# Second MLP's first GEMM by Strassen's seven products inside a block, in pairs of tiles

## The chip, the cores and the metric

One core of a Trainium2 chip. The time is that of one execution in device microseconds (us), the median of three runs. TensorE does the matrix products (PE in the profile, PEld for its weight loads); VectorE (DVE), ScalarE (ACT) and GpSimd (POOL) do the elementwise work; SyncE (SP) issues nearly all DMAs, in order, and a DMA that has to wait for a buffer or for data holds up those behind it.

## The reference, cut to what matters

Chunked attention on 4,608 tokens, then two MLPs, all float32. The change is about the second MLP, whose inputs are `x` (4608 x 512), `w_in` (512 x 2048) and `w_out` (2048 x 512):

```
h = x @ w_in
P = a0 + a1*h + a2*h^2 + a3*h^3
Q = 1 + |b0|*|h| + |b1|*h^2
out = (P / (Q + 1e-6)) @ w_out
```

## The kernel before

Every float32 operand of a product is kept as a pair (high part, rest) in TensorE's reduced float32, and each product runs as three matmuls: high by high, high by rest, rest by high (`PASSES`). "A product" below means such three passes.

The 4,608 tokens are nine blocks of 512 columns (`W`). The phases follow one another on TensorE:

* Attention and the first MLP's two input GEMMs: three blocks directly (`cell`), six blocks as three pairs of blocks by Strassen's seven products (`group`, tiles `sa`, `sb`). Attention for later blocks is woven in.
* The output pass of the first MLP: one block directly (tile `a`), eight blocks as four pairs by seven products (tiles `oa`, `ob`), written as 90 items of 12 matmuls. Operands are prepared three items ahead (`LEAD`): ACT takes the high part (L789), DVE the rest (L796).
* The second MLP (from `p2_first`): 144 steps, nine blocks by 16 tiles of 128 rows of h. A step is 12 matmuls 512 columns wide for h (`gemm1`, L428), an elementwise chain on the 128 x 512 tile, and, three steps later, 12 matmuls 512 columns wide of the output GEMM (L956) into four accumulators.

The elementwise chain of a step: ACT squares h (L925), takes |h| (L926) and a3*h+a2 (L927); DVE makes three operations from these (L928 to L930, the last two read h from PSUM); ACT takes a logarithm and an exponential (L936, L937) for the reciprocal; DVE does a Newton step and the product (L938, L939, L940; every tensor operand of these three lies in SBUF, as those of L928 do). Then ACT copies the high part (L945) and GpSimd subtracts to get the rest (L946). All these queues are written out by hand, in program order.

The next block's input is loaded from DRAM in four tiles of 128 x 512, each split by an ACT copy (L583) and a GpSimd subtraction (L584). The 32 tiles of the second MLP's weights are read as 64-bit words and turned into pairs while earlier phases run (`stage`: 18 of them in the Strassen groups, 14 in the output pass), written to DRAM, and read once into eight buffers of 2 MB (`unit2`) at the start of the second MLP, where they stay for all nine blocks. So in that phase next to nothing is loaded. The large buffers are 11 slabs of 16 KB per partition; small tiles of 512 columns come from a ring of 17 (`s2`).

## Time and profile before

| | us |
|---|---|
| time, median of 3 runs (lowest to highest) | 1717.96 (1717.67 to 1718.62) |
| the profiled execution | 1715.83 |
| its span, first to last instruction | 1714.0 |
| TensorE busy | 1681.1 (98%) |
| VectorE busy | 1365.1 (80%) |
| ScalarE busy | 1052.5 (61%) |
| GpSimd busy | 266.1 (16%) |

The mean granted TensorE clock is 0.999 of full speed. The profile's time for a matmul covers more than the distance to the next one, since matmuls overlap; the pace is read from the starts of consecutive groups.

### The profile page before, as it was taken

To read this page: it belongs to the slowest core of one execution; us is meant where nothing else is said; L and a number is where in the kernel's file an instruction comes from. 1 tells how busy PE (TensorE), PEld (TensorE's weight loads), DVE (VectorE), ACT (ScalarE), POOL (GpSimd) and SP (SyncE) were. 2 spreads that over 40 slices of the span, in tenths; PEclk is the share of its full clock that TensorE was granted. 3 is DMA by queue.
4 is the path that set the end of the run, shared out by engine and by line. 5 is a ranking of instruction groups with operands and counts; after the bars stand their busy time and mean duration, and the time that the engine had idled before them with its cause. 6 is when DMAs were issued, how large, how long until landed. Compare 5 with 4: busy or idle time off the path is not lost.

```text
span 1714.0 us, 25378 instructions
## 1 busy us (share of the span) xinstructions
PE 1681.1 (98%) x9600; PEld 1380.6 (81%) x9600; DVE 1365.1 (80%) x1961; ACT 1052.5 (61%) x1687; POOL 266.1 (16%) x258
## 2 busy tenths in 40 slices
PE   6899999999999999999999999999999999999998
PEld 5678877878878878888888888888888888888887
DVE  6868787777778679997885988887878787878786
ACT  6834345555555564565555877676767776767675
POOL 1000000000000000000002323232323232323222
PEclk9999999999999999999999999999999999999999
DMA  7875678877977998468648300010101010101000
GB/s 283 293 236 172 204 240 295 301 280 280 359 281 263 356 345 311 129 216 261 221 144 331 147 27 23 17 33 7 43 7 44 1 50 1 50 1 50 1 25 25
DMA packets 102442, 272.19 MB, mean 159 GB/s; under 512 B 10672, under 2 KB 32176, under 8 KB 97072
## 3 DMA queue, kind: packets, MB, share of 16 engines
q1 hardware_dynamic: 102176, 270.32, 44.5%
q8 instruction: 75, 1.23, 0.3%
q14 instruction: 47, 0.39, 0.1%
q10 hardware_dynamic: 144, 0.26, 0.0%
HBM read 184.55 MB, written 85.98 MB: 158 GB/s over the span
## 4 chain that ended last, share of the span: by engine, by line
PE 58%; issue 2%; POOL 1%; ACT 0%; DVE 0%; POOLq 0%; DVEq 0%
PE o L956 21%; PE h L428 21%; PE oa L889 8%; PE ob L889 6%; PE a L871 2%; POOL ggring L946 1%; POOLq L1054 0%; ACT L986 0%; DVE rring L796 0%; DVE T L930 0%; DVE V L928 0%; ACT R L936 0%; ACT R L937 0%; DVE V L938 0%; DVE V L939 0%
## 5 line engine op out<-in xcount | busy, mean ns | idle before, releaser
L428 PE MATMUL h<-x,w 128*128 128x512 f32 x1728 | 414.9, 389 | 0.9 <-DVE T L930 0.9
L956 PE MATMUL o<-w,ggring 128*128 128x512 f32 x1728 | 414.9, 389 | 0.1
L428 PEld LDWEIGHTS h<-x,w 128*128 128x128 f32 x1728 | 324.3, 188 | 68.6 <-DVE T L930 1.3
L956 PEld LDWEIGHTS o<-w,ggring 128*128 128x128 f32 x1728 | 324.2, 188 | 67.7 <-POOL ggring L946 0.5
L946 POOL TENSOR_TENSOR ggring<-T,ggring 128x512 fp32r<-128x512 f32 x144 | 187.3, 1301 | 517.4 <-ACT ggring L945 292.0
L925 ACT ACTIVATE V<-h 128x512 f32<-128x512 f32 x144 | 85.9, 597 | 170.3 <-PE h L428 169.7
L928 DVE SCALAR_TENSOR_TENSOR V<-V,small,R 128x512 f32<-128x512 f32 x144 | 108.3, 752 | 84.9 <-ACT R L926 84.9
L789 ACT CAST rring<-uring 128x1024 fp32r<-128x1024 f32 x90 | 94.5, 1053 | 87.4 <-PE ob L889 32.7
L938 DVE SCALAR_TENSOR_TENSOR V<-V,R 128x512 f32<-128x512 f32 x144 | 99.9, 694 | 47.0 <-ACT R L937 47.0
L796 DVE TENSOR_TENSOR rring<-uring,rring 128x1024 fp32r<-128x1024 f32 x90 | 109.5, 1221 | 28.6 <-ACT rring L789 27.9
L939 DVE SCALAR_TENSOR_TENSOR V<-V,R 128x512 f32<-128x512 f32 x144 | 123.9, 861 | 4.9
L584 POOL TENSOR_TENSOR x<-x2r,x 128x512 fp32r<-128x512 f32 x36 | 47.9, 1333 | 436.3 <-ACT x L583 433.5
L927 ACT ACTIVATE T<-h,small 128x512 f32<-128x512 f32 x144 | 112.6, 782 | 0.0
L940 DVE SCALAR_TENSOR_TENSOR T<-T,small,V 128x512 f32<-128x512 f32 x144 | 108.3, 752 | 5.1
L428 PE MATMUL g<-xT,w 128*128 128x512 f32 (+1 forms) x444 | 109.1, 391 | 3.1 <-ACT w L104 1.3
L930 DVE SCALAR_TENSOR_TENSOR T<-T,small,h 128x512 f32<-128x512 f32 x144 | 107.7, 748 | 5.1
L465 PE MATMUL sa<-right,left 128*128 128x512 f32 x432 | 109.9, 393 | 0.0
L465 PE MATMUL sb<-right,left 128*128 128x512 f32 x432 | 108.2, 392 | 0.2 <-ACT c L493 0.2
L428 PE MATMUL v<-xT,w 128*128 128x512 f32 (+1 forms) x444 | 107.5, 388 | 0.0
L937 ACT ACTIVATE R<-R,small 128x512 f32<-128x512 f32 x144 | 104.5, 726 | 4.7
L936 ACT ACTIVATE R<-V,small 128x512 f32<-128x512 f32 x144 | 106.0, 736 | 1.6
L945 ACT CAST ggring<-T 128x512 fp32r<-128x512 f32 x144 | 90.0, 625 | 18.3 <-DVE T L940 18.3
(155 smaller groups left out, 2640.6 us busy)
## 6 DMA issues: line engine op xcount, KB each, us to landing
left<-wsd SPq DMA_DIRECT2D x30, 2048.0 KB, 9.8
ud<-u SPq DMA_DIRECT2D x108, 256.0 KB, 3.2
uring<-ud SPq DMA_DIRECT2D x54, 512.0 KB, 5.4
raw<-in_w_dram SPq DMA_DIRECT2D x36, 512.0 KB, 6.4
w<-w2d SPq DMA_DIRECT2D x8, 2048.0 KB, 15.6
wsd<-cb SPq DMA_DIRECT2D x48, 256.0 KB, 2.8
raw<-in_w_dram SPq DMA_DIRECT2D x10, 1024.0 KB, 9.9
wsd<-w SPq DMA_DIRECT2D x36, 256.0 KB, 3.4
```

The source lines that it names most:

```text
L428: nc.tensor.matmul(out=acc[:, ts], lhsT=w[:, wh, wk], rhs=x[:, kk, xh, ts], start=kk == 0 and n == 0, stop=kk == KD - 1 and n == 2,)
L465: nc.tensor.matmul(out=acc, lhsT=lhs[:, wh, kk * P:(kk + 1) * P], rhs=rhs[:, kk, xh, :], start=start and kk == 0 and m == 0, stop=kk == 1 ...
L796: nc.vector.tensor_tensor(out=lo, in0=u_of(t, n, f), in1=hi.bitcast(F32), op=ALU.subtract)
L889: nc.tensor.matmul(out=banks[m][on], lhsT=w[:, wh], rhs=(lo if xh else hi)[:, k], start=fresh and f + k == 0 and p == 0, stop=f + k == KH ...
L927: nc.scalar.activation(out=T, in_=h, func=AF.Identity, scale=a3, bias=a2)
L928: nc.vector.scalar_tensor_tensor(out=V, in0=V, scalar=absb1, in1=R, op0=ALU.mult, op1=ALU.add)
L930: nc.vector.scalar_tensor_tensor(out=T, in0=T, scalar=a1, in1=h, op0=ALU.add, op1=ALU.mult)
L936: nc.scalar.activation(out=R, in_=V, func=AF.Ln, scale=TWO_M63, bias=lnb)
L939: nc.vector.scalar_tensor_tensor(out=V, in0=V, scalar=-2.0, in1=R, op0=ALU.add, op1=ALU.mult)
L940: nc.vector.scalar_tensor_tensor(out=T, in0=T, scalar=a0, in1=V, op0=ALU.add, op1=ALU.mult)
L946: nc.gpsimd.tensor_tensor(out=r[:, 1, :], in0=T, in1=r[:, 0, :].bitcast(F32), op=ALU.subtract)
L956: nc.tensor.matmul(out=acc2[j][m], lhsT=r[:, rh, ms], rhs=wt["q", f][:, wh, :], start=f == 0 and n == 0, stop=f == NF2 - 1 and n == 2,)
```

## The change

* **h in pairs of tiles.** Two neighbouring tiles of h (256 rows) by the block's 512 columns become a 2 x 2 matrix of 128 x 256 pieces; the contraction's 512 rows are cut in two as well. Instead of 24 matmuls 512 wide, a pair takes seven products of 6 matmuls each, 256 wide: 42 matmuls (`products2`). A pair's h lies in two PSUM banks, and there are two such tiles. Some products accumulate in PSUM on others, and three copies on ACT (`both_` twice, `p5`, 256 wide) and two additions on DVE (512 and 256 wide, PSUM in and out) do the rest.
* **The elementwise chain** runs on 1024 columns at a time, once per pair; the copy and subtraction of the output GEMM's operand (`ggring`) stay 512 wide, two each per pair.
* **Order.** TensorE's order is now written by hand too. Iteration p holds the products of pair p, the chain of pair p-1, the operand copies of pair p-2, and the 24 output matmuls of pair p-3 in three lots of eight (`others`): product 0, eight, products 1 to 3, eight, products 4 and 5, eight, product 6.
* **Weights.** `w_in` is kept in DRAM as the seven left operands of each pair of tiles (`wld`, made by `stage_left`, 8 of them: one in the direct cells, seven in the Strassen groups), 1,792 KB for a pair, and `load_lefts` reads them again for each of the 72 pairs into two buffers in turn. The 16 tiles of `w_out` are staged in the output pass (`stage`) and stay in four buffers.
* **The block's input** is loaded as four quarters (`fetch_x2`), turned into seven right operands: four DVE subtractions (`x2_sum`) and seven splits of an ACT copy and a GpSimd subtraction each, 512 columns (`x2_split`), at places in the block's eight iterations that `plan2` lists.
* **Joints.** The first two items' operands of the output pass are prepared in the last turns of the Strassen groups (`open_o`, `start_o`). The last six items of the output pass run as the lots of eight of the first three iterations (`EARLY`, `last_items`), and PSUM is divided once for both.

```diff
+PAIRS = (2, 3, 2)
+EARLY = 3
+BLOCK0 = (
+    (-20, "fetch", 0), (-18, "ring", 0), (-17, "split", 0, "B11"), (-16, "split", 0, "B21"), (-15, "sum", 0, "T1"),
+    (-14, "split", 0, "T1"), (-14, "sum", 0, "T3"), (-12, "ring", 1), (-11, "split", 0, "B22"), (-10, "sum", 0, "T2"),
+    (-10, "split", 0, "T3"), (-9, "split", 0, "T2"), (-9, "sum", 0, "N4"), (-8, "split", 0, "N4"), (-9, "lefts", 0),
+    (-6, "lefts", 1), (-6, "work"), (-3, "lefts", 2), (-3, "quad", 0), (-2, "gg"),
+)
...
+    def stage_left(g):
+        one, two = (raw_tile(4 * g + 2 * n) for n in range(2))
+        yield
+        yield from words_to_whole(*one)
+        yield from words_to_whole(*two)
+        x, y = (w[0].bitcast(F32) for w in (one, two))
...
+        yield from put(0, x, "a")
+        yield from put(6, y[:, W // 2:], "d")
+        a11, a12, a21, a22 = (z[:, k * W // 2:(k + 1) * W // 2] for z in (x, y) for k in range(2))
+        for o, i, j, op in ((a22, a21, a22, ALU.add), (a21, a11, a21, ALU.subtract), (a11, a22, a11, ALU.subtract), (a12, a12, a11, ALU.subtract)):
+            nc.vector.tensor_tensor(out=o, in0=i, in1=j, op=op)
+            yield
+        yield from put(2, x, "s")
+        yield from put(4, y, "u")
...
+    def x2_split(j, name):
...
+        nc.scalar.copy(hi, x)
+        nc.gpsimd.tensor_tensor(out=lo, in0=x, in1=hi.bitcast(F32), op=ALU.subtract)
+
+    def load_lefts(p):
+        parts = (slice(0, 7),)
...
+        if p < 3:
+            ring["lefts", p % 2] = slab(f"lefts{p}", (P, 8, 2, 2 * P))
+            parts = (slice(0, 3), slice(3, 7))
+        for part in parts:
+            nc.sync.dma_start(out=ring["lefts", p % 2][:, part].bitcast(F32), in_=wld[p % NPR][:, part])
...
+    def last_items():
+        for i in range(len(items) - 2 * EARLY, len(items)):
+            prepare(i)
+            todo = list(item_products(i))
+            for n, of in enumerate(todo):
+                nc.tensor.matmul(**of)
+                if n + 1 == len(todo):
+                    item_end(i)
+                yield
...
+        plan2 = ((0, "fetch", None), (2, "split", "B11"), (2, "split", "B22"), (2, "sum", "T1"), (3, "split", "B21"), (3, "sum", "T3"),
+                 (4, "split", "T1"), (4, "sum", "T2"), (5, "split", "T2"), (6, "sum", "N4"), (7, "split", "T3"), (7, "split", "N4"))
+
+        for p in range(NPAIR + 3):
+            a = p if p < NPAIR else None
+            b = p - 1 if 0 <= p - 1 < NPAIR else None
+            c = p - 2 if 0 <= p - 2 < NPAIR else None
+            if a is not None:
+                if p > 1 and p + 1 < NPAIR:
+                    load_lefts(p + 1)
+                tiles[p] = two_banks([P, 2, W], f"h{p}")
+                products2(p, (0,))
+            if b is not None:
...
+                nc.scalar.activation(out=V, in_=H, func=AF.Square)
+            if a is not None:
+                both_ = s2([P, W], f"both{p}")
+                nc.scalar.copy(both_[:, :HW], tiles[p][:, 1, :HW])
+            others(p, 0)
+            if b is not None:
+                nc.scalar.activation(out=R, in_=H, func=AF.Abs, scale=b0)
+                nc.vector.scalar_tensor_tensor(out=V, in0=V, scalar=absb1, in1=R, op0=ALU.mult, op1=ALU.add)
+                nc.scalar.activation(out=T, in_=H, func=AF.Identity, scale=a3, bias=a2)
+                nc.vector.tensor_tensor(out=T, in0=T, in1=H, op=ALU.mult)
+                nc.vector.scalar_tensor_tensor(out=T, in0=T, scalar=a1, in1=H, op0=ALU.add, op1=ALU.mult)
+            if a is not None:
+                products2(p, (1, 2, 3))
+            if c is not None:
...
+                for e in range(2):
+                    es = slice(e * W, (e + 1) * W)
+                    nc.scalar.copy(r[:, 0, es], Tc[:, es])
+                    (nc.vector if c == NPAIR - 1 else nc.gpsimd).tensor_tensor(
+                        out=r[:, 1, es], in0=Tc[:, es], in1=r[:, 0, es].bitcast(F32), op=ALU.subtract
                     )
...
+            if a is not None:
+                nc.scalar.copy(both_[:, HW:], tiles[p][:, 1, :HW])
+                p5 = s2([P, HW], f"p5_{p}")
+                nc.scalar.copy(p5, tiles[p][:, 0, HW:])
+            others(p, 1)
+            if a is not None:
+                products2(p, (4, 5))
+                nc.vector.tensor_tensor(out=tiles[p][:, 0], in0=tiles[p][:, 0], in1=both_, op=ALU.add)
+                nc.vector.tensor_tensor(out=tiles[p][:, 1, HW:], in0=tiles[p][:, 1, :HW], in1=p5, op=ALU.add)
+            if b is not None:
+                nc.scalar.activation(out=R, in_=V, func=AF.Ln, scale=TWO_M63, bias=lnb)
+                nc.scalar.activation(out=R, in_=R, func=AF.Exp, scale=-1.0, bias=expb)
+            others(p, 2)
+            if a is not None:
+                products2(p, (6,))
+            if b is not None:
+                nc.vector.scalar_tensor_tensor(out=V, in0=V, scalar=1.0 + 1e-6, in1=R, op0=ALU.add, op1=ALU.mult)
+                nc.vector.scalar_tensor_tensor(out=V, in0=V, scalar=-2.0, in1=R, op0=ALU.add, op1=ALU.mult)
+                nc.vector.scalar_tensor_tensor(out=T, in0=T, scalar=a0, in1=V, op0=ALU.add, op1=ALU.mult)
```

After these, `plan2`'s entries of the iteration follow, so its splits and sums stand last in the queues of ACT, GpSimd and DVE. At the end of a block (an iteration 2 of the next one) `others` also emits the four evictions of the output (L967, L969 before) and their DMAs, each behind its lot of eight.

## Rows read from the trace of the kernel before

**Rows 1.** Busy time by engine in stretches of 50 us: stretch, engines, clock, DMA share, GB/s.

```profile
600.00:650.00 50.00, 47.89 (x209) 38.58 (x208) 38.50 (x56) 31.44 (x48) 0.00 (x0) 1.00 0.94 343
...
850.00:900.00 50.00, 50.00 (x223) 41.38 (x222) 45.70 (x49) 29.08 (x37) 0.00 (x0) 1.00 0.48 168
...
1300.00:1350.00 50.00, 50.00 (x222) 41.39 (x222) 42.58 (x57) 35.80 (x58) 16.20 (x13) 1.00 0.01 2
```

**Rows 2.** Waits in the second MLP: waiter, releaser, us in total, times, longest.

```profile
PE h L428 <- DVE T L930: 0.9, 1, 0.9
```

**Rows 3.** Timeline of the second MLP, in order of time: start, us, instructions.

```profile
1301.33 1.29 POOL L584 TENSOR_TENSOR x<-x2r,x 128x512 fp32r<-128x512 f32 x1 [0.68 <-PE h L428]
...
1301.50 1.67 DVE L939 SCALAR_TENSOR_TENSOR V<-V,R 128x512 f32<-128x512 f32 x1
...
1303.90 2.88 PE L428 MATMUL h<-x,w 128*128 128x512 f32 x12
...
1306.62 2.88 PE L956 MATMUL o<-w,ggring 128*128 128x512 f32 x12
1306.82 0.60 ACT L925 ACTIVATE V<-h 128x512 f32<-128x512 f32 x1 [0.68 <-PE h L428]
1306.90 0.69 DVE L939 SCALAR_TENSOR_TENSOR V<-V,R 128x512 f32<-128x512 f32 x1
```

**Rows 4.** Timeline of TensorE near the start.

```profile
34.30 3.04 PE L428 MATMUL v<-xT,w 128*128 128x256 f32 x24
37.18 2.91 PE L428 MATMUL g<-xT,w 128*128 128x512 f32 x12
39.92 2.88 PE L428 MATMUL v<-xT,w 128*128 128x512 f32 x12
```

**Rows 5.** Busy time by engine in a stretch of those 256-wide matmuls.

```profile
35.50:36.10 0.60, 0.60 (x8) 0.60 (x6) 0.60 (x2) 0.07 (x1) 0.00 (x0) 1.00 1.01 353
```

**Rows 6.** Groups of ACT by line and shape: busy us, mean ns of one, idle before.

```profile
L927 ACT ACTIVATE T<-h,small 128x512 f32<-128x512 f32 x144 | 112.6, 782 | 0.0
L936 ACT ACTIVATE R<-V,small 128x512 f32<-128x512 f32 x144 | 106.0, 736 | 1.6
...
L926 ACT ACTIVATE R<-h,small 128x512 f32<-128x512 f32 x144 | 98.2, 682 | 0.0
L789 ACT CAST rring<-uring 128x1024 fp32r<-128x1024 f32 x90 | 94.5, 1053 | 87.4 <-PE ob L889 32.7 <-PE oa L889 29.3 <-PE a L871 10.2
L945 ACT CAST ggring<-T 128x512 fp32r<-128x512 f32 x144 | 90.0, 625 | 18.3 <-DVE T L940 18.3
L925 ACT ACTIVATE V<-h 128x512 f32<-128x512 f32 x144 | 85.9, 597 | 170.3 <-PE h L428 169.7
...
L323 ACT CAST right<-rawx 128x256 fp32r<-128x256 f32 x12 | 4.9, 407 | 17.2 <-DVE rawx L318 17.2
```

**Rows 7.** Groups of DVE by line and shape.

```profile
L796 DVE TENSOR_TENSOR rring<-uring,rring 128x1024 fp32r<-128x1024 f32 x90 | 109.5, 1221 | 28.6 <-ACT rring L789 27.9 <-PE ob L889 0.2 <-PE oa L889 0.2
...
L928 DVE SCALAR_TENSOR_TENSOR V<-V,small,R 128x512 f32<-128x512 f32 x144 | 108.3, 752 | 84.9 <-ACT R L926 84.9
...
L929 DVE TENSOR_TENSOR T<-T,h 128x512 f32<-128x512 f32 x144 | 98.3, 683 | 0.0
...
L497 DVE TENSOR_TENSOR c<-c,sb 128x512 f32<-128x512 f32 x72 | 48.5, 682 | 33.3 <-PE sb L465 25.8 <-DMA q<-in_qkv_dram 6.2 <-ACT u L437 0.7
...
L325 DVE TENSOR_TENSOR right<-rawx,right 128x256 fp32r<-128x256 f32 x12 | 5.0, 421 | 2.4 <-ACT right L323 2.4
```

**Rows 8.** The instructions of line 939: count, duration ns min/median/max.

```profile
L939 DVE SCALAR_TENSOR_TENSOR V<-V,R x144: 691/692/1675, 933.0 to 1703.0; 128x512 f32<-128x512 f32 x144
```

**Rows 9.** DMA issues: count, KB each, median us from issue to landing.

```profile
left<-wsd SPq DMA_DIRECT2D x30, 2048.0 KB, 9.8
...
w<-w2d SPq DMA_DIRECT2D x8, 2048.0 KB, 15.6
```

**Rows 10.** Timeline of TensorE's weight loads at the end.

```profile
1706.89 2.37 PEld L956 LDWEIGHTS o<-w,ggring 128*128 128x128 f32 x11 [0.47 <-POOL ggring L946]
```

More of the change, by code (lines that the diff above doesn't have):

```diff
@@ L99, in words_to_pair, with split @@
         yield
-        nc.vector.tensor_tensor(out=high, in0=high, in1=t, op=ALU.add)
+        for h, _, t in parts:
+            nc.vector.tensor_tensor(out=h, in0=h, in1=t, op=ALU.add)
         yield
-        x = high.bitcast(F32)
-        hi, lo = pair()
+    def split(x, hi, lo):
         nc.scalar.copy(hi, x)
         yield
-        (last or nc.vector).tensor_tensor(out=lo, in0=x, in1=hi.bitcast(F32), op=ALU.subtract)
+        nc.vector.tensor_tensor(out=lo, in0=x, in1=hi.bitcast(F32), op=ALU.subtract)
         yield
+    def words_to_pair(high, low, pair, wide=False):
+        yield from words_to_whole(high, low, wide)
+        yield from split(high.bitcast(F32), *pair())
     buffers = {}
@@ L559, in fused_kernel @@
     outs = [outs[n:n + U] for n in range(0, NF1, U)]
-    second = [(n, f) for f in range(NF2) for n in "iq"]
-    second = [second[n:n + U] for n in range(0, len(second), U)]
     TURN = [0]
@@ new lines, in fused_kernel, with fetch_x2, operand @@
+    NPR = NF2 // 2
+    ring = {}
+    quarter_of = {}
+    def fetch_x2(j):
+        for k in range(2):
+            for h in range(2):
+                x = s2([P, 2, HW], f"x2r{j}_{k}{h}")
+                nc.sync.dma_start(out=x, in_=x2d[j][:, 2 * k:2 * k + 2, h * HW:(h + 1) * HW])
+                quarter_of[j, k, h] = x
+    def operand(j, n):
+        at = (7 * j + n) % 12
+        return ring["x2"][at // 4][:, at % 4]
+    X2 = {"B11": 0, "B21": 1, "T2": 2, "T1": 3, "B22": 4, "T3": 5, "N4": 6}
@@ L878, in fused_kernel @@
[L878 to L879 removed]
+                        whole_acc[:] = [bank(f"a0_{m}") for m in range(KD)]
+                    for k, m in product_order(((k, m) for k in range(2) for m in range(KD)), f == NF1 - 2):
+                        ms = slice(m * P, (m + 1) * P)
+                        for p, (wh, xh) in enumerate(PASSES):
+                            yield dict(
+                                out=whole_acc[m],
+                                lhsT=wt["o", f + k][:, wh, ms],
+                                rhs=(lo if xh else hi)[:, k],
+                                start=f + k == 0 and p == 0,
+                                stop=f + k == NF1 - 1 and p == 2,
+                            )
@@ new lines, in item_products @@
+                    for k, m in product_order(((k, m) for k in range(2) for m in range(2)), f == KH - 2):
+                        w = left_o(LHS[n], f + k, m)
+                        for p, (wh, xh) in enumerate(PASSES):
+                            yield dict(
+                                out=banks[m][on],
+                                lhsT=w[:, wh],
+                                rhs=(lo if xh else hi)[:, k],
+                                start=fresh and f + k == 0 and p == 0,
+                                stop=f + k == KH - 1 and p == 2,
+                                skip_group_check=True,
+                            )
@@ new lines, in product_order, with item_end @@
+            def product_order(order, last):
+                return sorted(order, key=lambda km: km[1]) if last else order
+            def item_end(i):
+                t, n, f = items[i]
+                if t is None:
+                    if f == NF1 - 2:
+                        evict_plain(whole_acc)
+                elif f == KH - 2:
+                    evict(t, n, banks)
+                TURN[0] += 1
+            whole_acc, banks = [], []
+            for i in range(len(items) - 2 * EARLY):
+                prepare(i)
+                for of in item_products(i):
+                    nc.tensor.matmul(**of)
+                item_end(i)
```

402 lines of the change are left out of this document (208 added, 194 removed).

## The prediction

> **What bounds the kernel now.** I began with the busy times in stretches of 50 us. The second MLP has TensorE busy for 50.00 of 50.00 us, VectorE for 42.58, ScalarE for 35.80, and a DMA share of 0.01; in the output pass it is 50.00 too, with VectorE at 45.70; in the last Strassen groups it is 47.89, with a DMA share of 0.94 [rows 1]. Next the waits: in the whole second MLP TensorE waits once for VectorE, 0.9 us [rows 2]. So the phase that changes is set by the pace of the matmuls, and only fewer or shorter matmuls can shorten it. Last the timeline, for the pace: twelve matmuls 512 wide start at 1303.90 and the next twelve at 1306.62, so 2.72 us for twelve, 226.7 ns each [rows 3]. VectorE at 85% is the engine with the least room, so its queue has to be laid out too.
>
> **The gain: 42 matmuls 256 wide for 24 of 512.** Near the start the trace has 24 matmuls 256 wide with a weight load each, in one run: from 34.30 to 37.18, 2.88 us, 120.0 ns each [rows 4]. The granted clock is 1.00 in that stretch (the 2.4 GHz level) and the weight loads fill 0.60 of 0.60 us [rows 5]. The bounds: 113 ns, half of a 512-wide one; and 120.0, since the 24 ran beside a DMA share of 1.01 [rows 5] without a gap. I take 120.0, as the row is the same shape. A pair then costs 42 x 0.120 + 24 x 0.2267 = 5.04 + 5.44 = 10.48 us, against 48 x 0.2267 = 10.88 us. That is 0.40 us for each of 72 pairs, **28.8 us**. It is a third of what an eighth of the columns suggests: half-width matmuls cost 6 ns more than half. The Trainium skill (TensorE: Matmul & The Clock Gate, Back-to-back issue gap) gives a warm gap of N/2.4 + 2.5 ns: 109 ns for 256 and 216 for 512. By that rule a pair would save 0.64 us more than by the rows; the trace has 227 for 512, so I stay with the row.
>
> **Does everything else fit into 10.48 us?** TensorE's order in an iteration, from its start: product 0 to 0.72, lot one to 2.53, products 1 to 3 to 4.69, lot two to 6.51, product 4 to 7.23, product 5 to 7.95, lot three to 9.76, product 6 to 10.48.
>
> ScalarE: 428 ns for 512 more columns (1053 against 625) turn the five operations into 1.03 (square), 1.11, 1.21 and twice 1.16 us; with two copies of 0.625 and three of 0.407 that is 8.1 us a pair, and with 7/8 of a split 8.7 [rows 6]. In queue order: square from 0.20 (the first ScalarE read starts 0.20 after the next matmuls [rows 3]) to 1.2, first copy 1.6, |h| 2.7, a3*h+a2 3.9, operand copies 5.2, the other two copies 6.0, logarithm 7.2, exponential 8.3. Product 4 needs the copies at 6.51: 0.5 us to spare.
>
> VectorE: 538 ns for 512 more columns (1221 against 683). Three operations like L928 become 1.29, one like L929 1.22, two like L939 1.23 (692 + 538); the additions cost 0.68 and 0.42: 8.65 us, as much as the six narrow ones twice now [rows 7, 8]. The four sums (2.7 us a block) and evictions bring 9.2 a pair. In order: first operation 2.7 to 4.0, the next two to 6.5, additions 7.4 to 8.1 and 8.1 to 8.6 (after products 4 and 5), then three to 12.3, 1.8 us into the next iteration. Product 6 waits for the second addition, due at 9.76. The queue thus has three gaps, 0.9 before its first operation, 0.9 before the additions, 1.2 before product 6: **3.0 us of slack**. So the additions and wide operations cost nothing, as long as VectorE isn't held up by more than that.
>
> **What holds VectorE up.** At 1301.33 GpSimd starts a split's subtraction; L939, begun at 1301.50, takes 1.67 us instead of 0.69 and ends 0.55 us after GpSimd does [rows 3]. The median of L939 is 692, the longest 1675 [rows 8]. L929 and L930 beside L946 show nothing like that: they read PSUM. So an operation of VectorE with both tensors in SBUF and a GpSimd one exclude each other, at about 0.97 us each time. The Trainium skill states the same (SBUF — State Buffer, SBUF: two separate sides): the shared port pair is an exclusive lock, and whichever starts first keeps it for its whole instruction. The trace agrees; by the rule a meeting costs up to the full GpSimd operation, which gives the dearer case below.
>
> In an ordinary pair the operand subtractions start at about 4.6, beside the operations on PSUM: no meeting. But the splits of the next block's input stand behind the exponential, so they run from 8.5 on, exactly beside the three operations in SBUF. One split in an iteration (0.97) fits into 3.0. In a block's iteration 2 there are two splits, a sum (0.68) that stands behind them, the evictions (0.68 on VectorE in the way), and then the next operand subtraction meets the late first operation: 3 x 0.97 + 1.36 = 4.3, so product 6 of iteration 3 comes 1.3 us late; at the full 1.29 each it is 2.2, and if the meetings fall otherwise 0. Seven blocks have both splits and evictions: 0 to 15 us, and I take 1.2 each, **+8.5**, the measured price.
>
> **DMA.** 1,792 KB for each pair; 2048 KB landed in 9.8 us beside the Strassen groups' traffic, so 8.6; for the loads issued together it was 15.6, so 13.7 [rows 9]. The buffer comes free at an iteration's start and is needed 10.48 later. These loads are nearly alone in the queue now, so 8.6 is the nearer row: no cost. In iteration 2 the load stands on SP behind the last output DMA, 0.7 us more: it still fits.
>
> **The joints.** The start wait goes: -0.9 [rows 2]. In iteration 1 the load of pair 2's operands stands on SP behind two DMAs of the output pass, which wait for two additions on VectorE behind the first wide operations: issued some 8.2 us in, its first three of seven pieces (768 KB, 3.7 us by the 9.8 row, 5.9 by the 15.6 row) land at 11.9 to 14.1, against 10.48. 0 to 4, taken as **+2**. The last pair's chain after the last product runs against 2 x 5.44 us of output matmuls; now 0.47 is lost there [rows 10]; **+0.5** (0 to 1).
>
> **The other passes.** Each of eight weight pairs costs VectorE four subtractions of 256 columns and rests on 1792 columns instead of 1024: 4 x 0.42 + 1.1 = 2.8 us, 22 in all, over the 560 us before the output pass, where its busy share was 77% [rows 1]; the bytes are nearly the same. In the output pass two more tiles, four sums and seven splits instead of four go to a VectorE at 91%, with operands three items (8 us) ahead of TensorE. From -2 (the idle 2.1 us of the stretch at 600 vanish, as the last groups stage less) to +5: taken as **+1.5**.
>
> **Sum.** 1715.8 (the profiled execution; its span is 1714.0, so 1.8 lie outside) - 28.8 - 0.9 + 8.5 + 2 + 0.5 + 1.5 = 1698.6. The median is 2.1 above the profiled execution: **1701**, 1% below.
>
> **Rivals and chances.**
> * The forecast, a good microsecond lost a block: 0.47, 1696 to 1706.
> * No loss at the blocks, if the splits land in VectorE's gaps: 1692. For it: the meetings of now cost TensorE nothing [rows 2]. Chance 0.22.
> * Full-length meetings, 2.2 us a block, and a late start: 1708 to 1712. Chance 0.12.
> * 256-wide matmuls at half of 512-wide ones in a long run, 113 ns, since the 24 were the first dense ones: 42 x 0.007 x 72 = 21 us less, 1680. Against it: the weight loads filled that stretch. This is what the skill's gap rule points to. Chance 0.05.
> * Nothing gained, because the passes before lose what this one wins: 14 us or more there, from VectorE's 91% and the DMA share of 0.94. 1715. Chance 0.05.
> * Slower: VectorE becomes the bound, because the two operand subtractions of GpSimd (1.30 each) meet the first wide operation in every pair, not only at the blocks. 9.2 + 2.6 = 11.8 us a pair, 95 us over the forecast's 10.48, about 1787. It decides from 1.7 us of holding a pair, where VectorE's queue passes the 10.88 of now. Against it: the first operation starts at 2.7, the subtractions at 4.6. Chance 0.06.
> * Slower: each weight load lands later than 10.48; at 13.7 that is 3.2 a pair and 1920. It decides at 10.9. Chance 0.03.
>
> Faster by over 0.2% (which is about what a measurement of this kernel can tell from no change): 0.47 + 0.22 + 0.12 + 0.05 = 0.86. Within: 0.05. Slower: 0.09. The range, 1687 to 1713, holds the first three cases with the bounds of the joints.
>
> **What the new profile should show.** Groups of products starting 0.72 us apart for six; iterations of 10.48 us within a block; TensorE's only regular waits at product 6 of each block's iteration 3, for a VectorE addition behind operations of 2 us and more; weight loads landing in 7 to 9 us; VectorE at some 88% in the phase, DMA at some 180 to 200 GB/s (1.84 MB per 10.48 us and the rest); about 760 us for the phase instead of 785. The prediction is wrong if six 256-wide matmuls don't take 0.72 us, if waits stand in every pair, or if the Strassen groups or the output pass grow by more than 5 us.

## The result and the profile after

The changed kernel took 1701.45 us (median of four runs, 1701.2 to 1702.96) against 1717.82 us beside it: ratio 0.9909, 95% interval 0.9892 to 0.9927. The forecast was 1701. The profiled execution is the slowest of the four, 1702.96 us with a span of 1701.2.

The busy times in stretches of 50 us answer to [rows 1]. TensorE is still the full engine in the second MLP, VectorE went from 42.58 to 43.23, the DMA share from 0.01 to 0.54. Of the idle 2.1 us of the stretch at 600, 0.2 are left.

```profile
600.00:650.00 50.00, 49.82 (x220) 40.78 (x219) 41.10 (x67) 30.46 (x50) 0.00 (x0) 1.00 0.89 333
...
1300.00:1350.00 50.00, 50.00 (x315) 45.23 (x314) 43.23 (x42) 36.53 (x52) 20.34 (x14) 1.00 0.54 201
```

The waits of TensorE in the second MLP, which answer to [rows 2] (waiter, releaser, us in total, times, longest). They stand once a block: seven for ScalarE's copy `p` ahead of product 4, and one, in the first block, for VectorE's addition ahead of product 6. The waits for that addition in the other blocks are so short that this view, whose ends of matmuls are modelled, doesn't list them; the starts below show them.

```profile
PE h L1051 <- ACT p L1142: 2.3, 7, 0.3
PE h L1051 <- DVE h L1147: 1.2, 1, 1.2
```

An ordinary iteration on TensorE, in order of time (start, us, instructions; it answers to [rows 3, 4]). The start of the next group is the measure, since ends are modelled. Products 4 and 5 stand together (x12), and so do product 6 of one pair and product 0 of the next: 1.43 us each. Eight output matmuls: 1.84. Products 1 to 3 (x18): 2.15. From 1015.80 the pieces are 1.43, 1.84, 1.43, 1.85, 2.15 and, for the last eight (cut off by the end of this view; the next group starts at 1026.34), 1.84: 10.54 us.

```profile
1015.80 1.60 PE L1051 MATMUL h<-x2ring,lefts 128*128 128x256 f32 x12
1017.23 2.00 PE L1070 MATMUL o<-w,ggring 128*128 128x512 f32 x8
1019.07 1.60 PE L1051 MATMUL h<-x2ring,lefts 128*128 128x256 f32 x12
1020.50 2.00 PE L1070 MATMUL o<-w,ggring 128*128 128x512 f32 x8
1022.35 2.31 PE L1051 MATMUL h<-x2ring,lefts 128*128 128x256 f32 x18
1024.50 1.78 PE L1070 MATMUL o<-w,ggring 128*128 128x512 f32 x7
```

By the starts of products 1 to 3 all iterations are 10.53 to 10.56 us long but nine: iteration 3 of the first block 11.97, that of the other seven blocks with a successor 11.54 each, and one of 10.72. The timeline around such an iteration 3, the second block's:

```profile
1029.19 0.68 DVE L1086 TENSOR_SCALAR ob<-o 128x512 f32<-128x512 f32 x1
...
1031.00 3.52 POOL L645 TENSOR_TENSOR x2ring<-x2r,x2ring 128x512 fp32r<-128x512 f32 x2 [4.35 <-ACT x2ring L644]
1031.04 2.34 DVE L1156 SCALAR_TENSOR_TENSOR work<-work 128x1024 f32<-128x1024 f32 x1
...
1033.41 2.19 DVE L1157 SCALAR_TENSOR_TENSOR T<-T,small,work 128x1024 f32<-128x1024 f32 x1
...
1035.05 2.00 PE L1070 MATMUL o<-w,ggring 128*128 128x512 f32 x8
1035.52 0.68 DVE L638 TENSOR_TENSOR x2r<-x2r,x2r 128x512 f32<-128x512 f32 x1
1035.64 1.14 ACT L1135 CAST ggring<-T 128x512 fp32r<-128x512 f32 x2 [0.90 <-DVE T L1157]
...
1036.95 0.37 ACT L1142 COPY p<-h 128x256 f32<-128x256 f32 x1
...
1037.37 1.69 PE L1051 MATMUL h<-x2ring,lefts 128*128 128x256 f32 x12 [0.32 <-ACT p L1142]
...
1038.90 2.00 PE L1070 MATMUL o<-w,ggring 128*128 128x512 f32 x8
...
1041.05 1.49 PEld L1051 LDWEIGHTS h<-x2ring,lefts 128*128 128x128 f32 x12 [0.57 <-DVE h L1147]
1041.05 1.70 PE L1051 MATMUL h<-x2ring,lefts 128*128 128x256 f32 x12
```

GpSimd's two split subtractions run from 1031.00 to 1034.5. Beside them VectorE's L1156 takes 2.34 and L1157 2.19, against 1.23 and 1.28 in other pairs (the minimum and the median of L1156's 72 are 1224 and 1226 ns, the longest 2341). T is therefore 2 us late; ScalarE waits 0.90 for it, so its operand copies and, behind them, `p` are late. Product 4 starts at 1037.37, where 1035.05 + 1.84 = 1036.89 was due: 0.48. Product 6 starts at 1041.05, where 1038.90 + 1.84 = 1040.74 was due: another 0.31 for the addition L1147. The rest of the 1.00 is a third cost: each twelve matmuls that begin with a wait take longer from start to start (1.53 and 1.54) than those without (1.43), 0.1 us each.

In the first block, which has no output of the second MLP to evict, three VectorE operations in a row are long: L1157 2.20, the sum L638 1.78, and L1124 2.31. The last one meets GpSimd's next operand subtraction, which here began 0.19 us ahead of it; product 6 then waits 1.16 us for the addition.

```profile
949.58 3.67 POOL L1136 TENSOR_TENSOR ggring<-T,ggring 128x512 fp32r<-128x512 f32 x2 [0.28 <-ACT ggring L1135]
949.77 2.31 DVE L1124 SCALAR_TENSOR_TENSOR work<-work,small 128x1024 f32<-128x1024 f32 x1
```

The page's part on DMA issues, against the estimate of 8.6 us made from [rows 9]: 7.4.

```profile
lefts<-wld SPq DMA_DIRECT2D x69, 1792.0 KB, 7.4
```

The end, TensorE's weight loads (answers to [rows 10]): 0.46 + 0.21 + 0.22 + 0.28 = 1.17 idle ahead of loads, against the 0.47 of before.

```profile
1687.05 4.42 PEld L1070 LDWEIGHTS o<-w,ggring 128*128 128x128 f32 x20 [0.46 <-POOL ggring L1136]
1691.68 0.30 PEld L1070 LDWEIGHTS o<-w,ggring 128*128 128x128 f32 x2 [0.21 <-ACT ggring L1135]
1692.20 0.53 PEld L1070 LDWEIGHTS o<-w,ggring 128*128 128x128 f32 x3 [0.22 <-ACT ggring L1135]
1693.01 4.18 PEld L1070 LDWEIGHTS o<-w,ggring 128*128 128x128 f32 x19 [0.28 <-DVE ggring L1136]
```

### The profile page after: what moved, and what is told of

It is laid out like the page before. It is cut to its first block, busy times and chain, and to the rows that moved or that the text cites. A ratio compares the mean times of both kernels' runs of the same rounds, so it can differ in the third digit from the quotient of the medians.

```text
span 1701.2 us, 28101 instructions
## 1 busy us (share of the span) xinstructions
PE 1664.7 (98%) x10896; PEld 1418.6 (83%) x10896; DVE 1416.1 (83%) x1765; ACT 1060.2 (62%) x1592; POOL 330.2 (19%) x283
## 4 chain that ended last, share of the span: by engine, by line
PE 78%; DVE 13%; issue 4%; ACT 3%; DMA 2%; POOL 0%; SPq 0%; DVEq 0%; ACTq 0%
PE o L1070 20%; PE h L1051 19%; PE sa L512 9%; PE sb L512 7%; PE ob L1022 6%; PE oa L1022 6%; PE g L475 4%; PE v L475 3%; PE xs L270 1%; DMA k<-in_qkv_dram 1%; DVE work L1156 1%; PE a L1022 1%; PE tp L333 1%; DVE u L485 1%; DVE h L1146 1%
## 5 line engine op out<-in xcount | busy, mean ns | idle before, releaser
L1051 PEld LDWEIGHTS h<-x2ring,lefts 128*128 128x128 f32 x2982 | 384.5, 191 | 26.6 <-DVE h L1147 6.0
L1051 PE MATMUL h<-x2ring,lefts 128*128 128x256 f32 x2982 | 392.8, 283 | 4.4 <-ACT p L1142 2.3
L645 POOL TENSOR_TENSOR x2ring<-x2r,x2ring 128x512 fp32r<-128x512 f32 x63 | 99.4, 1589 | 446.5 <-PE oa L1022 360.6
L1117 ACT ACTIVATE work<-h 128x1024 f32<-128x1024 f32 x72 | 74.0, 1028 | 159.8 <-PE h L1051 147.5
L1156 DVE SCALAR_TENSOR_TENSOR work<-work 128x1024 f32<-128x1024 f32 x72 | 103.8, 1442 | 2.5
L1157 DVE SCALAR_TENSOR_TENSOR T<-T,small,work 128x1024 f32<-128x1024 f32 x72 | 99.8, 1386 | 2.5
L475 PEld LDWEIGHTS g<-xT,w 128*128 128x128 f32 x444 | 82.5, 194 | 20.4 <-ACT w L121 1.9
L1155 DVE SCALAR_TENSOR_TENSOR work<-work 128x1024 f32<-128x1024 f32 x72 | 95.6, 1327 | 0.3 <-ACT work L1150 0.3
L512 PEld LDWEIGHTS sb<-right,left 128*128 128x128 f32 x432 | 80.3, 188 | 17.0 <-DVE u L485 0.2
L1127 DVE SCALAR_TENSOR_TENSOR T<-T,small,h 128x1024 f32<-128x1024 f32 x72 | 92.2, 1281 | 2.5
L512 PEld LDWEIGHTS sa<-right,left 128*128 128x128 f32 x432 | 79.8, 188 | 17.2 <-DVE u L532 0.8
```

The lines of the kernel that those rows point to most:

```text
L475: nc.tensor.matmul(out=acc[:, ts], lhsT=w[:, wh, wk], rhs=x[:, kk, xh, ts], start=kk == 0 and n == 0, stop=kk == KD - 1 and n == 2,)
L512: nc.tensor.matmul(out=acc, lhsT=lhs[:, wh, kk * P:(kk + 1) * P], rhs=rhs[:, kk, xh, :], start=start and kk == 0 and m == 0, stop=kk == 1 ...
L645: nc.gpsimd.tensor_tensor(out=lo, in0=x, in1=hi.bitcast(F32), op=ALU.subtract)
L1051: nc.tensor.matmul(out=out_, lhsT=lhs[:, wh, kk * P:(kk + 1) * P], rhs=rhs[:, kk, xh, :], start=start and kk == 0 and m == 0, stop=kk == 1 ...
L1155: nc.vector.scalar_tensor_tensor(out=V, in0=V, scalar=1.0 + 1e-6, in1=R, op0=ALU.add, op1=ALU.mult)
L1156: nc.vector.scalar_tensor_tensor(out=V, in0=V, scalar=-2.0, in1=R, op0=ALU.add, op1=ALU.mult)
```

## The experiments

The time agreed with the forecast. That left open whether its two large terms were right for the reasons given: a phase at TensorE's pace, and some 1.2 us lost a block because GpSimd's splits hold VectorE up. Besides, an iteration took 10.54 us, not 10.48, and the earlier passes cost more than was forecast.

### One split moved away

```diff
-plan2 = ((0, "fetch", None), (2, "split", "B11"), (2, "split", "B22"), (2, "sum", "T1"), ...
+plan2 = ((0, "fetch", None), (1, "split", "B11"), (2, "split", "B22"), (2, "sum", "T1"), ...
```

> The split of B11 for the next block moves from the end of the third pair of a block to the end of the second; nothing else changes. In the changed kernel the iteration after the third pair took 11.54 us in place of 10.54 in each block, beside two GpSimd subtractions, two evictions and a sum. Theory A (the two GpSimd subtractions hold up the VectorE operations with both inputs in SBUF): with one of them gone from there about 1.0 us per block of VectorE time is given back, the iteration comes to 10.5 to 10.7, and the time to 1694 to 1696. Rival B (the evictions and the order of ScalarE's copies make the loss): the iteration stays at 11.4 to 11.6 and the time at 1701.

1693.15 us (ratio 0.9858, 0.9842 to 0.9875). Iteration 3 took 10.62 in seven blocks and 10.82 in the first. The timeline of the same block: one long VectorE operation is left, and the next has its usual length.

```profile
1027.46 1.30 POOL L645 TENSOR_TENSOR x2ring<-x2r,x2ring 128x512 fp32r<-128x512 f32 x1 [4.21 <-ACT x2ring L644]
1027.49 2.34 DVE L1156 SCALAR_TENSOR_TENSOR work<-work 128x1024 f32<-128x1024 f32 x1
...
1029.87 1.28 DVE L1157 SCALAR_TENSOR_TENSOR T<-T,small,work 128x1024 f32<-128x1024 f32 x1
```

Theory A's numbers, or a little better. Rival B falls as it stood: the evictions are where they were. But the split's copy on ScalarE moved along with its subtraction, so this run alone can't tell the two engines apart; the next runs can. In its new place the split runs beside the two additions, which work on PSUM, and L1155 takes 1.36 there in place of 1.22.

### Two further GpSimd subtractions, free to run early

```diff
+if p % NPR == 2:
+    for k in range(2):
+        x = operand(p // NPR, k)[:, :, 0].bitcast(F32)
...
+        nc.gpsimd.tensor_tensor(out=spare, in0=x, in1=x, op=ALU.subtract)
```

> Two further GpSimd subtractions of the size of the splits, both inputs in SBUF and their output read by nobody, stand at the end of the third pair of each block ahead of the two splits; no ScalarE or VectorE operation is added. Theory A: each costs VectorE another 1.0 us or so there, the iteration after goes from 11.54 to about 13.5, and the time rises by 2.0 x 7 or 8 blocks = 14 to 16 us, to 1715 to 1718. Rival B: VectorE is not held up, the iteration stays at 11.5, and the time within 3 us of 1701 (the splits themselves come later on GpSimd, but no product waits for them until some five pairs on).

1701.7 us, iterations as in the changed kernel. This looks like rival B, but the timeline shows that it tested nothing: the added subtractions waited for nobody and ran from 1025.69 to 1027.73. VectorE was idle for most of that time (1.36 us up to 1027.13) and then worked on PSUM.

```profile
1025.69 2.04 POOL L1170 TENSOR_TENSOR spare<-x2ring 128x512 f32<-128x512 f32 x2
...
1027.13 0.70 DVE L1146 TENSOR_TENSOR h<-h,both 128x512 f32<-128x512 f32 x1 [1.36 <-PE h L1051]
```

### The same two, tied to the splits

```diff
+if a is not None and p % NPR == 2 and p // NPR + 1 < NB:
+    for k, n in enumerate(("B11", "B22")):
+        x = operand(j, X2[n])[:, :, 0].bitcast(F32)
...
+        nc.gpsimd.tensor_tensor(out=spare, in0=x, in1=x, op=ALU.subtract)
```

> As the run with two further GpSimd subtractions, but these read what ScalarE writes for the two splits and so can't run before them; in that run they ran 3 us ahead, where VectorE waited for TensorE. In the changed kernel the two VectorE operations beside the splits took 2.34 and 2.19 us in place of 1.23 and 1.28. Theory A: the next two VectorE operations with both inputs in SBUF wait as well, some 2.0 us more in each of seven or eight blocks, the iteration after the third pair goes from 11.54 to 13 to 13.6 us, and the time to 1712 to 1718. Rival B: VectorE goes on, the iteration stays at 11.5 and the time at 1701 to 1703.

1722.21 us, 1.0026 of the kernel before (1.0017 to 1.0035): the whole gain is undone. Iteration 3 took 14.7 us in six blocks, 13.17 in the eighth and 11.72 in the first. Four VectorE operations in a row are now long, L1156 and L1157 as before, and the sum L638 (1.79 in place of 0.68) and L1124 (2.06 in place of 1.28) too; TensorE waits 2.04 for the addition behind them:

```profile
1029.76 2.33 DVE L1156 SCALAR_TENSOR_TENSOR work<-work 128x1024 f32<-128x1024 f32 x1
...
1034.00 1.79 DVE L638 TENSOR_TENSOR x2r<-x2r,x2r 128x512 f32<-128x512 f32 x1
...
1035.71 2.06 DVE L1124 SCALAR_TENSOR_TENSOR work<-work,small 128x1024 f32<-128x1024 f32 x1
...
1041.42 2.83 PE L1051 MATMUL h<-x2ring,lefts 128*128 128x256 f32 x12 [2.04 <-DVE h L1147]
1044.04 2.42 PE L1070 MATMUL o<-w,ggring 128*128 128x512 f32 x8
...
1572.41 1.69 PE L1051 MATMUL h<-x2ring,lefts 128*128 128x256 f32 x12 [2.04 <-DVE h L1147]
1573.94 2.00 PE L1070 MATMUL o<-w,ggring 128*128 128x512 f32 x8
```

No VectorE or ScalarE work was added, so rival B falls here too. The loss is larger than expected (3.2 a block, not 2), and half of it isn't VectorE's: in six blocks, behind this wait of 2.0 us, TensorE's granted clock falls from 1.00 to 0.50 (the 1.2 GHz level) for 3.4 us, from 1041.55 to 1044.96 in the block shown. Matmuls take 1.5 us more in it: here the twelve behind the wait take 2.62 from start to start and the eight after them 2.26. In the eighth block, the last two rows, the wait is the same 2.04, the clock stays at 1.00, the twelve take 1.53, and the iteration 13.17. So VectorE's delay alone costs 1.6 us a block over the 11.54, within theory A's 13 to 13.6 us; the six drops of the clock add 6 x 1.5 = 9 of the 20.8 us. All eleven runs of this kernel show the lower mean clock, 0.991 to 0.993. The trace of the changed kernel has no such drop in the second MLP before its last microsecond.

### The splits on VectorE

In the function of the split:

```diff
-nc.gpsimd.tensor_tensor(out=lo, in0=x, in1=hi.bitcast(F32), op=ALU.subtract)
+nc.vector.tensor_tensor(out=lo, in0=x, in1=hi.bitcast(F32), op=ALU.subtract)
```

> All subtractions of the splits of the second MLP's right sides run on VectorE in place of GpSimd, in the same places. Each is an operation on 128x512 with both inputs in SBUF, which for the sums took 0.68 us. Theory A: what VectorE loses to a split falls from about 1.0 to 0.68 us, two of them in the critical iteration, so it takes 10.9 to 11.1 in place of 11.54, and the time is 1697 to 1699. Rival B: nothing held VectorE up, so 1.36 us are added to a full engine, the iteration takes 12.5 to 12.9, and the time is 1708 to 1711.

1695.29 us (0.9868, 0.9853 to 0.9883), theory A and better than its 1697. Iteration 3 took 10.70 to 10.72, 11.81 in the first block (a load, see the last run). L1156 has its 1.23 again, and the two splits are one group of 1.29:

```profile
1029.88 1.23 DVE L1156 SCALAR_TENSOR_TENSOR work<-work 128x1024 f32<-128x1024 f32 x1
...
1032.34 1.29 DVE L645 TENSOR_TENSOR x2ring<-x2r,x2ring 128x512 fp32r<-128x512 f32 x2
```

VectorE does more work and is done earlier: two subtractions cost it 1.29 when it does them itself and 1.11 + 0.91 = 2.02 when GpSimd does them beside it. Moreover, they now stand behind T, so ScalarE's copies are not late.

### Only the sum moved

```diff
-... (2, "split", "B22"), (2, "sum", "T1"), (3, "split", "B21"), (3, "sum", "T3"), ...
+... (2, "split", "B22"), (3, "split", "B21"), (3, "sum", "T1"), (3, "sum", "T3"), ...
```

> Only the sum T1 of the next block (0.68 us of VectorE) moves from the end of a block's third pair to the end of the fourth; both splits and both evictions stay where they are. Theory A' (the iteration after the third pair is late by what VectorE has there beyond its slack: 2.0 us from two splits, 1.36 from two evictions, 0.68 from this sum, so any relief counts by its size): the iteration goes from 11.54 to 10.8 to 10.9, and the time falls by 7 to 8 x 0.68 = 5 us, to 1696 to 1697. Rival J (only the splits matter, by when they stand): 11.5 and 1701.

1707.66 us, some 6 more than the changed kernel and outside both forecasts. Iteration 3 fell to 11.12 to 11.18, 0.4 of the 0.68 (product 4's wait for ScalarE stays). But iteration 4, ordinary before, took 11.65 in all seven later blocks. Its timeline:

```profile
1044.76 1.41 DVE L638 TENSOR_TENSOR x2r<-x2r,x2r 128x512 f32<-128x512 f32 x2
...
1045.63 3.94 POOL L1136 TENSOR_TENSOR ggring<-T,ggring 128x512 fp32r<-128x512 f32 x2 [4.45 <-ACT ggring L1135]
...
1046.09 2.31 DVE L1124 SCALAR_TENSOR_TENSOR work<-work,small 128x1024 f32<-128x1024 f32 x1
```

In the changed kernel L1124 started 0.26 to 0.30 us ahead of GpSimd's operand subtraction in iterations 3 and 4 (1036.13 against 1036.39, 1045.82 against 1046.11; not in the first block's iteration 3): it took 1.27 or 1.28, and GpSimd's two took 3.4 in place of 2.6. Here the second sum lets GpSimd be first by 0.46, and L1124 takes 2.31. The price is paid by whoever comes second. The Trainium skill (SBUF — State Buffer, SBUF: two separate sides) has the same rule, that the first keeps the shared port for its whole instruction; both orders of the same two instructions in these two runs agree with it, 1.28 against 2.31. This is the mechanism of the rival that I had put at 1787 us. It did not come in every pair: in the changed kernel L1124 is 0.9 to 1.7 us ahead in ordinary pairs. But in two pairs of a block only 0.3 us in the order of two queues kept it away, and once, in the first block, they didn't.

### Both moved

```diff
-... (2, "split", "B11"), (2, "split", "B22"), (2, "sum", "T1"), (3, "split", "B21"), (3, "sum", "T3"), ...
+... (1, "split", "B11"), (2, "split", "B22"), (3, "split", "B21"), (3, "sum", "T1"), (3, "sum", "T3"), ...
```

> Both moves together: the split of B11 to the end of the second pair, the sum T1 to the end of the fourth. With the split alone an iteration a block kept 0.08 us, and the first block 0.28. Theory A': VectorE is within its slack everywhere, all iterations take 10.54 to 10.6, and the time is 1692 to 1693. Rival K: two sums and a split at the end of the fourth pair make the iteration after it late instead, 10.8 or more in each block, and the time is 1694 to 1696.

1699.92 us, slower than with the split alone. Iteration 3 took 10.54 in each block, and the one after it 11.33 to 11.36 in seven: rival K's place, with more than its price.

### Five lots of output matmuls

```diff
+LOTS = (0, 4, 8, 16, 20, 24)
...
-for e, m, n in todo[8 * part:8 * part + 8]:
+for e, m, n in todo[LOTS[part]:LOTS[part + 1]]:
...
```

The order is product 0, 4 output matmuls, product 1, 4, products 2 and 3, 8, product 4, 4, product 5, 4, product 6.

> The 24 matmuls of the second GEMM of a pair go in five lots (4, 4, 8, 4, 4) between the products 0, 1, 2 and 3, 4, 5, 6, in place of three lots of 8; the same matmuls in all. Theory A (changing from 256-wide to 512-wide matmuls and back costs about 0.026 us a lot: a lot of eight took 1.84 us where eight times 0.2267 is 1.81): two more lots make an ordinary iteration 10.60 in place of 10.54, and the time 1705 to 1706 (72 pairs). Rival C (the 512-wide matmuls are slower throughout this phase, 0.230 each, whatever stands beside them): the iteration stays at 10.54 and the time at 1701 +- 1.

1750.5 us (1.019, 1.0175 to 1.0205): 49 us slower, outside both. The second half of an iteration on TensorE:

```profile
1075.47 2.00 PE L1072 MATMUL o<-w,ggring 128*128 128x512 f32 x8
1077.31 0.88 PE L1051 MATMUL h<-x2ring,lefts 128*128 128x256 f32 x6
1078.02 1.09 PE L1072 MATMUL o<-w,ggring 128*128 128x512 f32 x4
1078.95 0.87 PE L1051 MATMUL h<-x2ring,lefts 128*128 128x256 f32 x6
1079.66 1.08 PE L1072 MATMUL o<-w,ggring 128*128 128x512 f32 x4
1081.22 1.69 PE L1051 MATMUL h<-x2ring,lefts 128*128 128x256 f32 x12 [0.48 <-DVE h L1155]
```

With four output matmuls behind product 5 instead of eight, VectorE's two additions are no longer covered: product 6 starts at 1081.22, where 1079.66 + 0.93 = 1080.59 was due. That is 0.63, and 0.11 for the slower twelve behind a wait (1069.93 to 1071.47 in the iteration before, 1.54): 0.74 in every iteration, 11.28 us from one such wait to the next. Times 71 that is 52.5; less 0.35 in each of seven iterations 3 and 1.4 in the first block's, which were late before, it is the 49 us. The changed kernel's third lot, the eight behind product 5, is that near to the edge. On the question itself: a lot of four takes 0.93 and one of eight 1.84, 0.02 to 0.03 over 0.2267 each, while a group of six products takes 0.71, 0.01 under its 0.72. Without the wait the iteration would sum to 10.55, so two more lots cost 0.01, not 0.05. Neither theory's price holds; the 0.06 us over 10.48 are too near the trace's 0.01 us to be put down to one term.

### Without the seventh product

```diff
-products2(p, (6,))
+pass
```

> The seventh product (A22 by N4) of all 72 pairs is left out; its operands are still loaded and made. Theory F (TensorE alone sets the pace, VectorE needs 9.2 of 10.54 us): an ordinary iteration is 0.72 us shorter, 9.82 us, the iteration after each third pair some 1.7 us more than that, and the time 1701.4 - 52 + 5 = 1654, between 1650 and 1660. Rival G (the chain of ScalarE and VectorE from a pair's products to its turn in the second GEMM stands close behind): an iteration keeps 10.2 us or more, and the time is 1675 to 1695.

1652.64 us (0.9619, 0.9606 to 0.9632). Iterations of 9.82 us: a product of TensorE taken away is 0.72 us gained at once, in 54 of 71 iterations. In the seven later blocks iteration 3 took 10.63 and the one ahead of it 10.33; in the first, three are longer. So theory F holds, and the next bound shows in two iterations a block. In both TensorE waits for a copy of ScalarE's:

```profile
1024.44 2.42 PE L1051 MATMUL h<-x2ring,lefts 128*128 128x256 f32 x18 [0.35 <-ACT both L1120]
...
1029.15 1.69 PE L1051 MATMUL h<-x2ring,lefts 128*128 128x256 f32 x12 [0.45 <-ACT p L1142]
```

The first copy stands behind an eviction, the two split copies and the square in ScalarE's queue; the second stands behind the operand copies, which wait 0.90 for VectorE's T, late beside the splits (2.34 and 2.20).

### The last items of the output pass ahead of the second MLP

```diff
-EARLY = 3
+EARLY = 0
```

> The last six items of the output pass run ahead of the second MLP and not between the products of its first three pairs. Theory H (without them the first three iterations hold 5.1 us of products each and wait for VectorE's and ScalarE's 9 us): iterations 2 and 3 take 8.5 to 9.5 us with 3.5 to 4.5 of it idle, and the first has the load of its operands less well covered: the time is 8 to 13 us longer, 1709 to 1714. Rival I (products run ahead, two pairs deep, and little is lost): 1702 to 1705.

1711.79 us, 10.3 more: theory H. The first two iterations took 8.59 and 8.59 us for 5.04 us of products. TensorE waits in each for both of ScalarE's copies and for the addition:

```profile
939.88 2.41 PE L1051 MATMUL h<-x2ring,lefts 128*128 128x256 f32 x18 [0.66 <-ACT both L1120]
943.02 1.70 PE L1051 MATMUL h<-x2ring,lefts 128*128 128x256 f32 x12 [0.74 <-ACT p L1142]
946.12 1.69 PE L1051 MATMUL h<-x2ring,lefts 128*128 128x256 f32 x12 [1.40 <-DVE h L1147]
```

### The first pair's operands made in the Strassen groups

```diff
-PAIRS = (2, 3, 2)
+PAIRS = (3, 3, 2)
...
-steps = stage_left(0)
-at_turn(B0[1] + 4, next, steps)
-spread(B0[1] + 8, steps, 1, 2, 12)
...
-for t, (many, before) in enumerate(zip(PAIRS, (1, 3, 6))):
+for t, (many, before) in enumerate(zip(PAIRS, (0, 3, 6))):
```

> The seven left operands of the first pair are made in the Strassen groups of the first GEMM with the others (3, 3, 2 a group of three) and no longer in the direct cells. In the changed kernel the direct cells ended 2.7 us later than before the change, 0.7 of it in a wait for VectorE at 163 us, where this work stands. Theory D (the load on VectorE): the direct cells end 0.7 to 2.0 us earlier, the Strassen groups lose at most 0.5, and the time is 1699.5 to 1701. Rival E (most of the 2.7 us comes with the granted clock of the first 150 us, 0.92 in a window where before had 1.00, and not from this work): the direct cells end within 0.8 us of the changed kernel, and the time is 1700.5 to 1702.

1705.08 us, 3.6 more, outside both ranges. The direct cells end no earlier (279.66 against 278.99, by the first matmul `sa`), while TensorE's wait of 0.67 at 163 us falls to 0.3. The Strassen groups grew to 387.6 us (667.21 - 279.66) from the 385.0 to 386.3 of the kernels whose groups are unchanged; the waits there are longer, for ScalarE's `p` 3.0 in place of 1.8 and for a load of `k` 1.6 in place of 1.0. So moving pair 0 did not pay. What it was worth to the direct cells one profile can't tell, as they end anywhere between 277.7 and 280.6 where their code is the same.

### The output pass with its work on VectorE spread

Beside both moves of split and sum:

```diff
-at = turn_o + 10 + n * (len(items) - 24) // NF2
+at = turn_o + 20 + n * (len(items) - 36) // NF2
-spread(turn_o + 3 + 3 * f // 2, left_sums(f), 1, 4, 3)
+spread(turn_o + 1 + 3 * f // 2, left_sums(f), 1, 4, 3)
```

> As the run with both moves, and in the output pass the sums of the left operands start two turns earlier and the unpacking of the second MLP's output weights starts at the pass's turn 20 in place of 10. In the changed kernel the pass took 2.4 us longer than before it, with waits of 0.5, 1.0 and 0.4 us of TensorE for VectorE at 666, 720 and 725 us, where VectorE was busy 47.85 of 50. Theory L (the added work on VectorE in the first third of the pass makes those waits): the waits at 720 and 725 go, the pass is 1.0 to 1.5 us shorter than in the run with both moves, and the time is 1.0 to 1.5 us less. Rival M: the planner puts VectorE's operations in much the same order, or the wait comes later in the pass: within 0.4 us of that run.

1698.97 us against 1699.92. The times can't tell these apart; the profile can. From its first matmul to the first product of the second MLP the pass took 246.07 us, against 248.10 in the run with both moves and 247.69 in the changed kernel: theory L, with 2.0 us in place of 1.0 to 1.5. The waits in the changed kernel's pass stand below; with the work spread only one of 0.4 us ahead of `a` is left.

```profile
PE oa L1022 <- DVE rring L854: 1.0, 1, 1.0
PE a L1022 <- DVE rring L854: 0.5, 1, 0.5
```

### The two edits that helped

```diff
-plan2 = ((0, "fetch", None), (2, "split", "B11"), (2, "split", "B22"), (2, "sum", "T1"), ...
+plan2 = ((0, "fetch", None), (1, "split", "B11"), (2, "split", "B22"), (2, "sum", "T1"), ...
...
-at = turn_o + 10 + n * (len(items) - 24) // NF2
+at = turn_o + 20 + n * (len(items) - 36) // NF2
-spread(turn_o + 3 + 3 * f // 2, left_sums(f), 1, 4, 3)
+spread(turn_o + 1 + 3 * f // 2, left_sums(f), 1, 4, 3)
```

> The changed kernel with the split of B11 at the end of the second pair (the sum T1 stays where it was) and the output pass's VectorE work spread as in the run before: the two edits that each took waits away. With the split moved alone the time was 1693.15; the spread took the wait at 720 us away and made the pass 1.6 to 2.0 us shorter. Theory N (the two lie in separate stages and add): the pass ends 1.5 to 2.0 us earlier, the iterations are those of the run with the split moved (10.62 once a block), and the time is 1691 to 1692.5. Rival O (the direct cells differ by up to 2.5 us between kernels whose code there is the same, so this may hide or double it): 1690 to 1695 with the pass still 1.5 to 2.0 us shorter.

1692.14 us (0.9851, 0.9834 to 0.9867), the lowest median of the study; its interval overlaps that of the moved split alone (1693.15), so a further gain in time is not shown. The profile shows it in its stage: the pass is 246.04 us long (664.37 to 910.41) against 247.81 with the split alone, and iterations 3 of the later blocks are 10.62. But the stages ahead of the pass ended 1.6 us later in this profile (664.37 against 662.76), as rival O allows. Theory N holds for the pass and the iterations. The first block's iteration 3 took 11.42 instead of 10.82; here TensorE waits for a weight load.

```profile
953.39 0.95 PE L1051 MATMUL h<-x2ring,lefts 128*128 128x256 f32 x6 [0.65 <-DMA lefts<-wld]
```

The run with the splits on VectorE has the same wait, 1.06 us, in the same place; in the changed kernel that iteration waited 1.16 for the addition instead. Why this one load is late was not tried.

## Why the prediction was right, point by point

* **The gain, 28.8 us.** The mechanism was right: fewer columns are less time in the whole phase, and the run with six products shows that nothing else sets the pace of an ordinary iteration. Eighteen 256-wide matmuls take 2.15, the 120 ns of the row near the start; the 113 ns of half a 512-wide one did not come out. The Trainium skill (TensorE: Matmul & The Clock Gate, Back-to-back issue gap) gives 109 ns by its formula, which it states for an isolated matmul; this trace, with a weight load before each, does not agree: 120. The prediction's sum from it was wrong as well: by 109 and 216 ns a pair saves 0.61, which is 0.21 more than by the rows, not 0.64. An eighth of the first GEMM's 5.44 us a pair is 0.68, so the 0.40 forecast were three fifths of it and not a third. The lots were under-sized: eight output matmuls take 1.84, not 1.81. An iteration is 10.54, and the gain 0.34 x 72 = 24.5: 4.3 us less than forecast.
* **Blocks, +8.5.** Measured: 7 x 1.00 + 1.43 + 0.18 = 8.6 (0.18 for the iteration of 10.72, whose cause was not sought). That the sum is so close is luck in part: the seven blocks cost 1.00 and not 1.2, and the 1.43 are the first block's, for which nothing was forecast. The cause, GpSimd's subtractions and VectorE operations with both tensors in SBUF excluding each other, is shown by four runs: with one split moved away 8.3 us come off the time, with the splits on VectorE 6, and with two more tied to them 11 to 12 are added beside 9 from the clock; in the run with only the sum moved, the order of two instructions turns 1.28 into 2.31. One step was wrong: I let all of it fall on product 6, with 0.5 us to spare for ScalarE's copies ahead of product 4. T is late as well, so half falls ahead of product 4. The meeting with the next operand subtraction (the third of 3 x 0.97) did not happen in these seven blocks, where L1124 came first by 0.26 us or more; it happened in the first block, and there the wait stands at product 6 as forecast.
* **Startup, +2.** Nothing: the iterations of the first pairs are 10.54 to 10.56. The load of pair 2's operands was not late; in three of the other kernels a load was, two iterations on, by 0.4 to 1.1 us. **Start wait, -0.9:** gone as forecast. **End, +0.5:** 0.7 more is idle ahead of weight loads (1.17 against 0.47); the last 72 matmuls themselves take 0.7 more than 72 x 0.2267 (17.14, less the 0.16 by which a group's modelled end exceeds its pace, against 16.32). So 0.2 to 0.7 up to the last matmul. Behind it the span goes on for 3.56 us (from 1697.61), 4.36 before (from 1709.68): 0.8 less, which was not forecast and not looked into. In all -0.6 to -0.1.
* **What the profile should show.** The phase took 768 us (1680.48 + 17.14 - 912.95, less the 16.3 of the output pass's items in it), not 760; VectorE stands at 86% in the stretch at 1300 (88 forecast) and the DMA at 201 GB/s (180 to 200).
* **DMA.** Landing in 7.4 us where 8.6 was estimated, and hidden in all pairs of the changed kernel.
* **Other passes, +1.5.** The output pass grew by 2.4 us (247.69 + 72 x 0.2267 for the items now in the second MLP = 264.0, against 924.64 - 663.01 = 261.6). 1.6 to 2.0 of it go when the sums of its left operands start earlier and the unpacking later; the two were not tried apart. The Strassen groups shrank, from 386.8 (663.01 - 276.24) to 386.3 in this profile and to 385.0 to 385.3 in ten of eleven others. The direct cells ended 2.7 us later in this profile, at 278.99; in eleven other profiles of kernels with this stage unchanged they end between 277.7 and 280.6, and the stretches of 20 us in which the granted clock is 0.91 or 0.92 differ among them: 20 to 40 us in the kernel before, 100 to 120 in the changed one, 40 to 60 in the one with the sum moved, and both 20 to 40 and 100 to 120 in the last. The kernel before and the changed one have one such stretch each, so the clock alone doesn't explain the 2.7. Only one profile of the kernel before exists, 2 us under its median, so whether this stage lost anything stays open.
* **The sum.** -24.5 - 0.9 + 8.6 + 2.4 = -14.4, with -0.6 to -0.1 for the end and -0.5 to -1.8 for the groups -15.0 to -16.8, against a measured -16.4 between the medians. The two profiled spans differ by 12.8 (1714.0 to 1701.2), and the stages give it: the direct cells +2.7, the groups -0.5, the pass +2.4, the second MLP up to its last matmul -16.7, and -0.8 behind it. The gain's shortfall (+4.3) on one side, the startup's (-2), the end's and the groups' on the other largely cancelled: the total was better than its terms, and that is luck.

## What to carry to other kernels

Before work is moved to an engine that looks idle, look at whose queue runs beside it: GpSimd at 19% cost more than the same subtractions on a VectorE at 83%, as two of them held VectorE up for 2.0 us where doing them itself took 1.3. Moving one of two splits by an iteration brought another 8.3 us, half of what the whole change had brought. A filler's position between two dependent pieces counts more than its number: four matmuls instead of eight behind product 5 cost 49 us. And an operation that comes first by 0.3 us is not safe there: any work put ahead of it may turn the order.

## What the hardware showed unexpectedly

* A wait of TensorE costs more than its length: the twelve matmuls behind it take 1.53 or 1.54 us from start to start instead of 1.43, in the changed kernel as in that with five lots. With two more subtractions tied to the splits it can cost more still: behind six of seven waits of 2.0 us the granted clock fell to 0.50 for 3.4 us, 1.5 us lost each time.
* 512-wide matmuls in lots between 256-wide ones take 0.02 to 0.03 us a lot more than in a long run (36 of the output pass stand 8.16 us apart, 226.7 ns each), and six 256-wide ones between lots 0.01 less than in a row.
